# Sliding-window attention and a gated feed-forward on one core: block 1 begun on three of its four tiles, tile 9 loaded ahead of wo, and unit 7's divisions put before masks

## The chip, the cores and the metric

The kernel runs on one core of a Trainium2 chip. The metric is the device time of one launch in microseconds (us). Before the change it is 340.84 us, the median of three runs that lie between 340.82 and 340.93 us.

## What is computed

Eight batches of causal attention with eight heads, 576 positions of 64 numbers, a window of 128 and a bias that falls with distance; then a gated feed-forward over all 4608 rows.

```python
q, k, v: (8, 8, 576, 64)            # batch, head, position, dim
scores = q @ k.T / 8 + slope[h] * -abs(i - j)
scores = where((i - j >= 0) & (i - j < 128), scores, -1e9)
attn   = softmax(scores) @ v
x      = attn.transpose(0, 2, 1, 3).reshape(4608, 512)
g      = x @ w_gate                 # 512 -> 1536
out    = (silu(g) * (x @ w_val)) @ w_out    # 1536 -> 512
```

Inputs and output are float32 in memory. The kernel converts the inputs to float16 while they are loaded, and accumulates in float32.

## The kernel before, in words

**Units and blocks.** Attention is done in 36 units: for each pair of batches eight tiles of 128 positions and one tile that holds the last 64 positions of both. A unit's x is 128 rows of 512. The feed-forward works on nine blocks of 512 rows. Block 0 takes units 0 to 3, block 1 units 4 to 7; unit 8 goes to the last block, and unit 9 opens the second pair of batches. For a block, `wide` (L394) forms for each of twelve slices of the hidden width a gate tile `pg` and a value tile `pv`: four matmuls of 128x512 each, over the four parts of the contraction. ScalarE then takes a tanh (L420), VectorE makes `uu` (L421) and multiplies by `pv` into `hT` (L432). Blocks 0 and 1 have `gate_val`'s two steps per slice, so 24 steps are block 0. Block 0 is projected with wo by `project` (L451, twelve matmuls per 128 rows); later blocks by a scheme with seven products instead of eight.

**One unit.** Its q and k tiles are loaded by GpSimd as 128 rows, transposed on TensorE (L214, the DMA's transpose from rank 11 on), and multiplied (L282, or L318 for the units with half-width tiles). ScalarE takes the exponential, VectorE multiplies by a mask (L294, L326). `weighted` (L330) multiplies by v into two halves `av` (L350) and divides: a reciprocal (L352) and a multiplication (L353) for each half. `x_transposed` (L363) transposes x on TensorE (`px`, L376), and ScalarE copies it into the block's `xT` (L380). With that a tile of the block is there.

**PSUM.** The eight banks are split: three for the tag "gv" (gate and value tiles after the start), one for "po" (projections of block 0), four for "a" (scores, av, transposes).

**Begun tiles.** Block 0's first four gate and value tiles are begun by `begin` (L819) on the columns of the tiles that are there: `wide` with a column limit leaves the half-made tile in `early`, and the later call computes only the columns that are left.

**What sets the order.** The loads on GpSimd's queue are in program order, written out by hand (L886 to L920): q, k, v tiles among the slices of the gate and value weights, then v of tile 8, then the two halves of wo (L913, L914; the second half of its rows first), then k and q of tile 9, q of tile 10 and the rest. TensorE, VectorE and ScalarE run in program order up to the eighth step of block 0. From there to step 60 the compiler's list scheduler chooses the order of each engine: it takes the earliest instruction in program order that its own model of time holds to be ready. After step 60 TensorE is again in program order. The order that results is fixed before the kernel runs; on the chip an engine that waits for one instruction doesn't go on to the next. Program order puts the whole chain of unit 7 and the scores of unit 8 ahead of block 1, since `ready` (L925) asks for eight finished units before the sixth step from the end of block 0.

Of the kernel before, what the change touches and what calls it, by code (L numbers as in the profile page):

```python
# [16 lines left out]
P = 128  # L17
# [21 lines left out]
def slot(h):  # L39

    return 4 * (h // 4) + 2 * (h % 2) + (h % 4) // 2
# [9 lines left out]
def kernel(  # L51
# [10 lines left out]
    nc = tc.nc  # L62
    B, H, S, D = q.shape
# [105 lines left out]
    def source(src, rank):  # L169

        s, c = divmod(rank, 9)
        if c == 8:
            return [((64 * n, 64 * n + 64),
                     src[2 * s + n, :, 512:576, :].rearrange("h p d -> p h d")) for n in range(2)]
        b, t = 2 * s + c // 4, c % 4
        return [((0, P), src[b, :, t * P:(t + 1) * P, :].rearrange("h p d -> p h d"))]

    def load_v(rank):
        va[rank] = va_all[rank % NV]
        for (p0, p1), src in source(v, rank):  # L180
            nc.gpsimd.dma_start(va[rank][p0:p1, :, 0:D], src)  # L181

    def load_qk(rank, which="kq"):
        for name in which:
            t_ = nat.tile([P, H, D], FP16, name=name + "n", tag=name + "n")
            for (p0, p1), src in source(k if name == "k" else q, rank):
                nc.gpsimd.dma_start(t_[p0:p1], src)  # L187
            (natk if name == "k" else natq)[rank] = t_

    def load(rank):  # L190
        load_qk(rank)
        load_v(rank)
# [137 lines left out]
    def weighted(i):  # L330

        s, p = units[i]
        x = xpool.tile([P, H, D], FP16, name="x", tag="x")
        xs[i] = x
        for half in range(2):
            pool, tag = (ps_f, "gv") if i < FIRST else (ps_a, "a")
            av = pool.tile([P, 4, D + 1], FP32, name="av", tag=tag)
            todo = []
            for j in range(4):
                h = 4 * half + j  # L340
                if p == 8:
                    for n, kt in enumerate((3, 7, 8)):
                        todo.append((j, ex[(s, "c", n)][:, slot(h), :], va[9 * s + kt][:, h, :]))
                else:
                    if p not in (0, 4):
                        todo.append((j, ex[(s, p - 1)][:, slot(h), 128:256],
                                     va[9 * s + p - 1][:, h, :]))
                    todo.append((j, ex[(s, p)][:, slot(h), 0:128], va[9 * s + p][:, h, :]))
            for n, (j, w, val) in enumerate(todo):
                nc.tensor.matmul(av[:, j, :], w, val, start=(n == 0), stop=(n == len(todo) - 1))  # L350
            rec = xpool.tile([P, 4, 1], FP32, name="rec", tag="rec", bufs=4)
            nc.vector.reciprocal(rec, av[:, :, D:D + 1])  # L352
            nc.vector.tensor_mul(x[:, 4 * half:4 * half + 4, :], av[:, :, 0:D],  # L353
                                 rec.broadcast_to([P, 4, D]))

    xT = {}

# [33 lines left out]
    early = {}  # L391
    OTHER = {(0, 0, "g"), (0, 0, "v"), (0, 1, "g"), (0, 1, "v")}

    def wide(n, m, which, c1=512):  # L394

        w, ms = wg_sb if which == "g" else wv_sb, slice(m * P, (m + 1) * P)
        ps, c0 = early.pop((n, m, which), (None, 0))
        if ps is None:
            pool, tag = (ps_a, "a") if (n, m, which) in OTHER else (ps_f, "gv")
            ps = pool.tile([P, 512], FP32, name="p" + which, tag=tag)  # L400
        for kb in range(NKB):
            nc.tensor.matmul(ps[:, c0:c1], w[:, kb, ms], xT[n][:, kb, c0:c1],  # L402
                             start=(kb == 0 and c0 == 0), stop=(kb == NKB - 1 and c1 == 512),
                             skip_group_check=(n == 0))
        if c1 < 512:
            early[(n, m, which)] = (ps, c1)
        return ps
# [87 lines left out]
    def at_once(fs):  # L495
        for f in fs:
            f()
# [208 lines left out]
    def ffn():  # L706

        for n in range(NBLK):
            if n > 1:
                parts = chain(strassen(n - 1, 0), strassen(n - 1, 1))  # L710
            if n == 1:
                for j in range(PRE):
                    for _ in project(0, j, ps_f, "po", 1):
                        yield 1.0
            if n == SEVEN_FROM:
                break
            due, given = 0, 0
            for m in range(NMB):
                for half, _ in enumerate(gate_val(n, m)):
                    scored[0] = False  # L720
                    yield 1.0
                    due += n > 1 and 2 * m + half in AT
                    while due and not (scored[0] and given % 7 == 1):
                        next(parts)
                        due, given = due - 1, given + 1
                        yield 0.75
                    if n > 1:
                        for _ in range(1 + (len(later) > 3)):
                            if later:
                                later.pop(0)()  # L730
                if n == 1:
                    if m in (4, 6, 8, 10):
                        for _ in project(0, m // 2 - 2, ps_f, "po", 1):
                            yield 1.0
                    if m in (4, 6, 8):
                        weight_sums(m // 2 - 2)
                if n > 0 and m >= 9:
                    (at_once if n == 1 and m < 11 else later.extend)(sums(n, m - 9))
                if n + 1 == SEVEN_FROM:
                    if m == SILU_AT:  # L740
                        attention_ends()
                        by_silu.update((n, i) for i in range(m + 1, NMB))
                    if m in (SILU_AT + 1, SILU_AT + 2):
                        later.extend(gate_val_weight_sums(m - SILU_AT - 1))
                    if m == SILU_AT:
                        later.extend(x_sums(n + 1))
            if n > 1:
                assert next(parts, 0) == 0
        ends = [strassen(NBLK - 1, t) for t in range(2)]
        tail = ExitStack()  # L750
        for n, k, name, which in seven_steps():
            if k == 0 and n > SEVEN_FROM:
                assert next(parts, 0) == 0
                parts = chain(strassen(n - 1, 0), strassen(n - 1, 1))
            if n == SEVEN_FROM and k in (1, 3, 10, 17):
                later.extend(gate_val_weight_sums(2 + (k + 4) // 7))
            yield 0.5
            if k % 3 == 2 and k < 42:
                next(parts)
                yield 0.75  # L760
            if k == 20 and n + 1 < NBLK:
                later.extend(x_sums(n + 1))
            if k == 35:
                later.extend(sums(n, 0))
            if name == "fourth" and which is not None and which[1] > 3:
                if n + 1 < NBLK or k < 39:
                    later.extend(sums(which[0], which[1] - 3))
            for _ in range(2 if len(later) > 4 or k < 7 else 1):
                if later:
                    later.pop(0)()  # L770
            if n == NBLK - 1 and k == 38:
                at_once(later)
                later.clear()
                tail.enter_context(tc.manual_schedule(engines={ET.DVE}))
            if n == NBLK - 1 and k == 39:
                one, two = sums(n, 1), sums(n, 2)
                one[0]()
            if n == NBLK - 1 and k == 41:
                one[1]()
                next(ends[0])  # L780
                yield 0.75
            if n == NBLK - 1 and k == 42:
                two[0]()
        assert next(parts, 0) == 0 and not later
        at_once((two[1], one[2], two[2], one[3], two[3]))

        for t in (1, 0, 1, 0, 1, 0, 1, 0, 0, 1, 0, 1, 1):
            next(ends[t])
            yield 0.75
        tail.close()  # L790
# [25 lines left out]
                f()  # L816
            yield

    def begin(n, tiles):  # L819

        for m, which in ((0, "g"), (0, "v"), (1, "g"), (1, "v"), (2, "g"), (2, "v"))[:n]:
            if early.get((0, m, which), (None, 0))[1] < tiles * P:
                wide(0, m, which, tiles * P)

    def first_tiles():

# [83 lines left out]
    load_w(1280, 1536)  # L910
    load_v(7)
    load(8)
    nc.gpsimd.dma_start(wo_sb[:, 6:12, :], wo2[:, 6:12, :])  # L913
    nc.gpsimd.dma_start(wo_sb[:, 0:6, :], wo2[:, 0:6, :])  # L914
    load_qk(9)
    load_qk(10, "q")
    load_v(9)
    load_qk(10, "k")
    load_v(10)
# [94 lines left out]
```

The softmax here doesn't subtract the row's maximum and nothing guards it: scores larger than these inputs give would overflow.

## Time and profile before

| engine | busy us | share of the span |
|---|---|---|
| TensorE matmuls | 328.6 | 97% |
| VectorE | 274.7 | 81% |
| ScalarE | 208.3 | 61% |
| GpSimd | 109.7 | 32% |

The profiled span is 339.4 us, with a mean granted TensorE clock of 0.997. The chain that ended last lies 79% on TensorE and 11% on DMA. The page gives each engine's busy time and then cuts the span in 40 slices; a stretch of the trace can be asked for the busy time of each engine in it, and the timeline gives each instruction's start, its length, and in brackets the idle time of the engine before it with what ended it. Idle time counts only on the engine that sets the end. A matmul's recorded length is longer than its share of the stream, since matmuls overlap: four of 128x512 take 0.86 us from the start of one group to the start of the next.

### The profile page before, as it was taken

To read this page: it belongs to the slowest core of one execution; us is meant where nothing else is said; L and a number is where in the kernel's file an instruction comes from. 1 tells how busy PE (TensorE), PEld (TensorE's weight loads), DVE (VectorE), ACT (ScalarE), POOL (GpSimd) and SP (SyncE) were. 2 spreads that over 40 slices of the span, in tenths; PEclk is the share of its full clock that TensorE was granted. 3 is DMA by queue.
4 is the path that set the end of the run, shared out by engine and by line. 5 is a ranking of instruction groups with operands and counts; after the bars stand their busy time and mean duration, and the time that the engine had idled before them with its cause. 6 is when DMAs were issued, how large, how long until landed. Compare 5 with 4: busy or idle time off the path is not lost.

```text
span 339.4 us, 7672 instructions
## 1 busy us (share of the span) xinstructions
PE 328.6 (97%) x2935; PEld 217.4 (64%) x2935; DVE 274.7 (81%) x643; ACT 208.3 (61%) x415; POOL 109.7 (32%) x136
## 2 busy tenths in 40 slices
PE   8999987999999999999999999999999999999994
PEld 4564444444455665566665655666688888888884
DVE  4668874999888779998899999999955885776683
ACT  4866774555575676666665647563467776776650
POOL 8977675377837068743008000000000000000000
PEclk9999999999999999999999999999999999999998
DMA  9999999999999999999939913021101101011014
GB/s 151 169 178 178 166 162 162 128 139 157 142 170 147 172 153 179 157 156 154 181 109 109 152 39 93 17 58 53 62 2 64 47 17 65 0 65 62 2 64 125
DMA packets 160037, 37.37 MB, mean 110 GB/s; under 512 B 147328, under 2 KB 155648, under 8 KB 160000
## 3 DMA queue, kind: packets, MB, share of 16 engines
q0 software_dynamic: 118336, 18.62, 80.3%
q1 hardware_dynamic: 40976, 17.64, 28.4%
q10 hardware_dynamic: 688, 0.62, 0.6%
q8 instruction: 23, 0.38, 0.5%
q14 instruction: 14, 0.11, 0.1%
HBM read 37.91 MB, written 9.44 MB: 139 GB/s over the span
## 4 chain that ended last, share of the span: by engine, by line
PE 79%; DMA 11%; POOL 4%; DVE 2%; ACT 2%; issue 1%; POOLq 0%
PE po L537 19%; PE pg L402 15%; PE pv L402 15%; PE gX L626 9%; DMA wv_sb<-in_moe_w_val_dram 5%; PE gY L626 5%; PE av L350 4%; DMA qn<-in_q_dram 3%; PE ps L282 3%; PE p L537 3%; DMA va<-in_v_dram 3%; PE gZ L626 2%; PE po L456 2%; POOL va L181 1%; PE px L376 1%
## 5 line engine op out<-in xcount | busy, mean ns | idle before, releaser
L402 PE MATMUL pv<-xT,wv_sb 128*128 128x512 f16 (+2 forms) x304 | 75.8, 368 | 0.3 <-DVE uu L421 0.3
L402 PE MATMUL pg<-xT,wg_sb 128*128 128x512 f16 (+2 forms) x304 | 75.1, 368 | 0.2 <-DVE xT L378 0.2
L420 ACT ACTIVATE tt<-pg 128x512 f16<-128x512 f32 x68 | 41.0, 603 | 47.2 <-PE pg L402 46.9
L288 ACT ACTIVATE ex<-ps 128x512 f16<-128x512 f32 x96 | 49.9, 606 | 7.5 <-PE ps L282 7.5
L421 DVE SCALAR_TENSOR_TENSOR uu<-tt,pg 128x512 f16<-128x512 f16 x67 | 45.6, 680 | 9.1 <-ACT tt L420 9.1
L432 DVE TENSOR_TENSOR hT<-uu,pv 128x512 f16<-128x512 f16 x68 | 46.2, 680 | 2.9 <-PE pv L402 1.3
L181 POOL DMA_DIRECT2D va<-in_v_dram x40 | 34.3, 865 | 42.3 <-PE av L350 34.6
L537 PEld LDWEIGHTS <-hT 128*128 128x128 f16 x384 | 37.2, 98 | 10.6 <-issue 0.8
L402 PEld LDWEIGHTS <-wv_sb 128*128 128x128 f16 x304 | 27.3, 98 | 24.8 <-issue 2.7
L402 PEld LDWEIGHTS <-wg_sb 128*128 128x128 f16 x304 | 27.3, 98 | 23.2 <-issue 1.9
L187 POOL DMA_DIRECT2D kn<-in_k_dram x39 | 33.3, 858 | 16.8 <-DMA qT<-qn 6.4
L187 POOL DMA_DIRECT2D qn<-in_q_dram x39 | 33.4, 865 | 12.6 <-DMA va<-in_v_dram 5.4
L537 PEld LDWEIGHTS <-S 128*128 128x128 f16 x288 | 27.4, 98 | 7.3 <-issue 1.4
L294 DVE TENSOR_TENSOR ex<-ex,m_reg 128x1024 f16<-128x1024 f16 x42 | 28.7, 685 | 2.6 <-ACT ex L288 2.5
L353 DVE TENSOR_TENSOR x<-av,rec 128x256 f16<-128x256 f32 x72 | 28.7, 419 | 0.4
L537 PE MATMUL po<-T,S 128*128 128x256 f16 x192 | 25.9, 273 | 0.3 <-ACT u2s L563 0.3
L537 PE MATMUL po<-T,hT 128*128 128x256 f16 x192 | 26.0, 272 | 0.0
L322 ACT ACTIVATE exc<-psc 128x512 f16<-128x512 f32 x40 | 21.3, 607 | 1.9 <-PE psc L318 1.9
L680 DVE TENSOR_TENSOR hT<-s,v 128x512 f16<-128x512 f16 x18 | 7.6, 424 | 17.7 <-ACT s L679 17.7
L350 PEld LDWEIGHTS <-ex 128*128 128x128 f16 x384 | 17.4, 97 | 3.9 <-issue 0.4
L350 PE MATMUL av<-va,ex 128*128 128x65 f16 x384 | 19.3, 193 | 0.0
L282 PE MATMUL ps<-qT,kT 64*128 64x256 f16 x192 | 16.9, 272 | 0.3 <-DVE qT L219 0.2
(130 smaller groups left out, 535.3 us busy)
## 6 DMA issues: line engine op xcount, KB each, us to landing
out_dram<-osb SPq DMA_DIRECT2D x32, 256.0 KB, 2.1
va<-in_v_dram POOLq DMA_DIRECT2D x32, 128.0 KB, 7.8
qn<-in_q_dram POOLq DMA_DIRECT2D x31, 128.0 KB, 8.1
kn<-in_k_dram POOLq DMA_DIRECT2D x31, 128.0 KB, 8.8
wg_sb<-in_moe_w_gate_dram POOLq DMA_DIRECT2D x6, 256.0 KB, 7.7
wv_sb<-in_moe_w_val_dram POOLq DMA_DIRECT2D x6, 256.0 KB, 8.1
wo_sb<-in_moe_w_out_dram POOLq DMA_DIRECT2D x2, 768.0 KB, 10.4
kn<-in_k_dram POOLq DMA_DIRECT2D x8, 64.0 KB, 6.0
```

The source lines that it names most:

```text
L181: nc.gpsimd.dma_start(va[rank][p0:p1, :, 0:D], src)
L187: nc.gpsimd.dma_start(t_[p0:p1], src)
L288: nc.scalar.activation(e[:, o:o + 2, :], banks[q4][par], AF.Exp, scale=scale)
L294: nc.vector.tensor_mul(e[:, o, :], e[:, o, :], reg[:, o, :])
L350: nc.tensor.matmul(av[:, j, :], w, val, start=(n == 0), stop=(n == len(todo) - 1))
L353: nc.vector.tensor_mul(x[:, 4 * half:4 * half + 4, :], av[:, :, 0:D], rec.broadcast_to([P, 4, D]))
L402: nc.tensor.matmul(ps[:, c0:c1], w[:, kb, ms], xT[n][:, kb, c0:c1], start=(kb == 0 and c0 == 0), stop=(kb == NKB - 1 and c1 == 512), skip_ ...
L420: nc.scalar.activation(tt, pg[:, c0:c1], AF.Tanh, scale=0.5)
L421: nc.vector.scalar_tensor_tensor(out=uu, in0=tt, scalar=one if (n, m) == PIN else 1.0, in1=pg[:, c0:c1], op0=ALU.add, op1=ALU.mult)
L432: nc.vector.tensor_mul(hT[n][:, m, c0:c1], acted[(n, m)][1][:, c0:c1], pv[:, c0:c1])
L537: nc.tensor.matmul(dst, a[:, m, cols], b[:, m, :], start=(start and m == 0), stop=(m == HM - 1), skip_group_check=True)
L626: nc.tensor.matmul(dst[:, i, :], w[:, kb, c0 + i * P:c0 + (i + 1) * P], a[:, kb, :], start=(start and i == 0 and kb == 0), stop=(i == 1 an ...
```

## The change

Three edits aim at the end of block 0, where the first two blocks meet. (1) When block 1 opens, three of its tiles (the gate and value tiles of slice 0 and the gate tile of slice 1) are begun on the 384 columns of units 4, 5 and 6. The last 128 columns follow when unit 7's x is there. (2) k and q of tile 9 and q of tile 10 are loaded ahead of wo instead of behind it. (3) The reciprocals and multiplications of unit 7 are given high priority in the scheduler, so that the mask multiplications of unit 8's scores don't come between them.

```diff
@@ weighted
             rec = xpool.tile([P, 4, 1], FP32, name="rec", tag="rec", bufs=4)
-            nc.vector.reciprocal(rec, av[:, :, D:D + 1])
-            nc.vector.tensor_mul(x[:, 4 * half:4 * half + 4, :], av[:, :, 0:D],
-                                 rec.broadcast_to([P, 4, D]))
+            with tc.high_priority() if i == 7 else ExitStack():
+                nc.vector.reciprocal(rec, av[:, :, D:D + 1])
+                nc.vector.tensor_mul(x[:, 4 * half:4 * half + 4, :], av[:, :, 0:D],
+                                     rec.broadcast_to([P, 4, D]))
@@ wide
-                             skip_group_check=(n == 0))
+                             skip_group_check=(n <= 1))
@@ ffn
             if n == 1:
+                begin(3, 3, 1)
@@ begin
-    def begin(n, tiles):
+    def begin(n, tiles, block=0):
 
         for m, which in ((0, "g"), (0, "v"), (1, "g"), (1, "v"), (2, "g"), (2, "v"))[:n]:
-            if early.get((0, m, which), (None, 0))[1] < tiles * P:
-                wide(0, m, which, tiles * P)
+            if early.get((block, m, which), (None, 0))[1] < tiles * P:
+                wide(block, m, which, tiles * P)
@@ the loads
     load(8)
+    load_qk(9)
+    load_qk(10, "q")
     nc.gpsimd.dma_start(wo_sb[:, 6:12, :], wo2[:, 6:12, :])
     nc.gpsimd.dma_start(wo_sb[:, 0:6, :], wo2[:, 0:6, :])
-    load_qk(9)
-    load_qk(10, "q")
     load_v(9)
```

## Prediction

> **What bounds the kernel now.** I read the page first, then the busy time by stretch, then TensorE's timeline where it is idle, then VectorE's there.
>
> From the page:
>
> ```profile
> span 339.4 us, 7672 instructions
> PE 328.6 (97%) x2935; PEld 217.4 (64%) x2935; DVE 274.7 (81%) x643; ACT 208.3 (61%) x415; POOL 109.7 (32%) x136
> ```
>
> TensorE is busy 97%, so 339.4 - 328.6 = 10.8 us of idle time is all that reordering could win. Where it lies, by stretch (columns: stretch, length, busy us and count of PE, PEld, DVE, ACT, POOL, then clock, DMA share, GB/s):
>
> ```profile
> 47.00:50.00 3.00, 1.86 (x29) 1.34 (x29) 2.25 (x6) 2.08 (x5) 1.38 (x2) 1.00 1.10 162
> 50.00:54.00 4.00, 2.99 (x32) 1.53 (x31) 2.94 (x7) 2.24 (x5) 0.88 (x1) 1.00 1.79 178
> 54.00:57.30 3.30, 2.48 (x22) 1.38 (x21) 0.68 (x2) 1.17 (x2) 2.86 (x4) 1.00 2.43 155
> 57.30:65.00 7.70, 7.70 (x38) 3.21 (x37) 6.01 (x12) 4.06 (x7) 1.51 (x2) 1.00 2.05 153
> ```
>
> From 47 to 57.3 us TensorE is idle 1.14 + 1.01 + 0.82 = 2.97 us, at full clock. From 57.3 to 338 us, asked as one stretch, it is busy 277.19 of 280.70 us. So what is won before 57.3 us should reach the end nearly whole. The timeline there (start, length, instruction; in brackets the idle time before it and what ended it):
>
> ```profile
> 49.97 0.38 PE L456 MATMUL po<-wo_sb,hT 128*128 128x512 f16 x1 [0.26 <-DMA wo_sb<-in_moe_w_out_dram]
> ...
> 53.78 0.59 PE L456 MATMUL po<-wo_sb,hT 128*128 128x512 f16 x2 [1.01 <-DMA wo_sb<-in_moe_w_out_dram]
> 54.21 0.27 PE L376 MATMUL px<-idm,x 128*128 128x128 f16 x2
> 54.74 0.40 PE L214 MATMUL pt<-idm,kn 128*128 128x128 f16 x4 [0.26 <-DMA kn<-in_k_dram]
> 55.70 0.40 PE L214 MATMUL pt<-idm,qn 128*128 128x128 f16 x4 [0.56 <-DMA qn<-in_q_dram]
> 55.94 0.59 PE L456 MATMUL po<-wo_sb,hT 128*128 128x512 f16 x2
> 56.37 0.28 PE L376 MATMUL px<-idm,x 128*128 128x128 f16 x2
> ...
> 57.32 1.02 PE L402 MATMUL pg<-xT,wg_sb 128*128 128x512 f16 x4
> ```
>
> Block 1 starts at 57.32 because its fourth tile is unit 7's x, whose second half of transposes (56.37) stands behind fillers that wait for DMA: projections of block 0 for wo, transposes of tile 9 for k and q. Four waits, 0.26 + 1.01 + 0.26 + 0.56 = 2.09 us, are for transfers that nothing urgent needs. VectorE at that time:
>
> ```profile
> 52.38 0.18 DVE L352 RECIPROCAL rec<-av 128x4 f32<-128x4 f32 x1 [0.28 <-PE av L350]
> 52.48 0.39 DVE L353 TENSOR_TENSOR x<-av,rec 128x256 f16<-128x256 f32 x1
> 52.79 0.68 DVE L326 TENSOR_TENSOR exc<-exc,m_c 128x1024 f16<-128x1024 f16 x1
> 53.39 0.42 DVE L353 TENSOR_TENSOR x<-av,rec 128x256 f16<-128x256 f32 x1
> ```
>
> A mask of 0.68 us stands between the two halves of unit 7's x.
>
> **What the skill says.** The Trainium skill's "TensorE: Matmul & The Clock Gate" ("Step-by-step: what each phase is for") says that matmuls stay in program order and only weight loads are pulled ahead. The trace agrees: px at 56.37 waits behind pt at 55.70, though x was done at 53.81. "DMA: Bandwidth & Descriptors" ("Queues, rings and completion order") says that each DMA engine consumes one ring's descriptors in order. The trace agrees: issue plus landing time gives wo's halves at 40.67 + 9.3 = 49.97 and 42.30 + 11.4 = 53.70, k of tile 9 at 43.12 + 11.6 = 54.7, then q of 9 and 10 at 55.7 and 56.6. "PSUM — Partial Sum Buffer" ("The four PSUM rules") allows one matmul at most one bank; so three tiles begun are all three "gv" banks, and the fourth has to wait for one.
>
> **The change, part by part.**
>
> *Splitting the three tiles.* Twelve matmuls of 512 columns become twelve of 384 and twelve of 128. In block 0 groups of four start 0.44 us apart at 256 columns and 0.22 at 128, in block 1 0.86 at 512: 110, 55 and 216 ns each. So 384 is about 163 ns, and 163 + 55 = 218 against 216: no cost, 12 x 2 ns. Twelve more weight loads (98 ns each) overlap; the groups at 128 columns show that they already do.
>
> *Whether the begun part may run before unit 7's x is written.* It reads columns 0 to 383 of xT and the copy writes 384 to 511, but the copy is earlier in program order. Block 0 shows that no false wait follows:
>
> ```profile
> 19.99 0.38 PE L376 MATMUL px<-idm,x 128*128 128x128 f16 x4 [0.52 <-DVE xT L378]
> 20.21 0.39 PE L402 MATMUL pg<-xT,wg_sb 128*128 128x128 f16 x4
> 20.41 0.42 DVE L378 COPY xT<-px 128x512 f16<-128x512 f16 x1 [0.47 <-PE px L376]
> ```
>
> The begun pg of tile 2 runs at 20.21, before the copy of tile 3 at 20.41. In block 1 the third tile (unit 6) is copied at 48.70 for 0.59 us, so from 49.3 on TensorE has 12 x 163 = 1.95 us of work that waits for no DMA. The "gv" banks are free by then: block 0's last pv starts at 46.50 and is read at 48.57 for 0.68 us.
>
> *Tile 9 ahead of wo.* The same bytes in another order. The three tiles are 0.95 us apart in landing, so wo's halves come 2.85 us later, at about 52.8 and 56.5, and k9, q9, q10 at about 47.1, 48.1 and 49.0 (wo's first half took 3.75 us of transfer, as the halves are 3.75 apart, so the slot begins near 46.2). The waits at 54.74 and 55.70 (0.82 us) go, and their 0.66 us of transposes can fill the idle time near 48. v9 and what follows land as before. GpSimd's queue gets no new wait that matters: its issues run 6 to 12 us ahead of landing.
>
> *Priority.* x's second half would start at about 52.8 and end at 53.2 instead of 53.81. The mask comes 0.35 us later; only unit 8 waits for it, which goes to the last block. Then px at about 53.4 and the copy (0.59) until about 54.3.
>
> *Sum.* From 49.34 to 57.32 there are 7.98 us, of which 2.09 are waits: 5.89 of work. Without the twelve projections (12 x 0.216 = 2.59) 3.30 remain; with the begun matmuls 3.30 + 1.95 = 5.25. So TensorE is done at about 54.6, just after x is there at 54.3, and block 1's rest starts 2.72 us earlier. It has 1.95 us done and 2.59 us of projection yet to do: net 2.72 + 1.95 - 2.59 = 2.08, the removed waits again.
>
> *The wait that it adds.* The fourth tile (pv of slice 1) wants a bank 12 x 0.055 = 0.66 us after the rest starts. Before, pg's first matmul started at 57.32 and uu, which frees the bank, ended at 59.76, 1.42 us after pg's end (58.34). Now pg's rest ends 0.39 us in, so the bank comes at 0.39 + 1.42 = 1.81: a gap of 1.15 us. What stands behind is all of block 1. Bounds: 0, if projections (2.59 us, if wo has landed) or scores of unit 9 (0.61 us, with k9 and q9 there) fill it; 1.15 if nothing does. I take 0.4.
>
> So 2.09 - 0.4 = 1.7 us: 340.84 - 1.7 = 339.1 us.
>
> **The rivals.**
>
> *A filler still waits for wo.* The scheduler placed projections ahead of px by a model that held wo to be there 0.3 to 1.0 us too early. If the first projections of the second half stay ahead of px, TensorE waits for wo until 56.5 instead of 53.78 and the rest starts about 58.2 (56.5 + 0.86 of projections and transposes + 0.8 for px and its copy). 1.95 us is done by then, 0.9 is lost: gain about 1.05, 339.8 us. For it: both waits for wo stand in the trace. Against: the begun tiles precede projections in program order.
>
> *The gain is given back in block 1.* The bank gap stays open (-1.15), and a wait of 0.7 us for wo: 2.09 - 1.85 = 0.2, 340.6 us. For it: VectorE is busy 14.67 of 15.00 us from 65 to 80, so it has no room to catch up on late evictions. Against: VectorE is busy only 0.68 us of 54.00 to 57.30 and could start the evictions some 3 us earlier.
>
> *Slower.* All orders after step 8 of block 0 come from one list schedule, and on VectorE and ScalarE to the end. TensorE's idle time after 57.3 is small (3.5 us with the tail), so a new order can hardly be better there and may be worse. If it opens the 1.15 us gap and waits as large as the largest now (1.01, and 0.82 for the two transposes), 2.98 us, the result is 340.84 - 2.09 + 2.98 = 341.7 us. For it: VectorE's share. Against: no such wait stands in TensorE's waits now; the longest after 57.3 is 0.3.
>
> **How the numbers follow.** First case 0.55 (339.1); waits for wo 0.18 (339.8); given back 0.16 (340.6); slower 0.11 (341.7). Within 0.2% is 340.16 to 341.52. The first two are faster, less a little that spills: 0.71; the third and the spill: 0.18; slower 0.11. The range reaches down to 338.3 (all of 2.09 and 0.4 more, from transposes in the idle 1.14 us near 48) and up to 341.0, through the third case.
>
> **What would show it.** Right: pg and pv of 128x384 from about 49.3; transposes of tile 9 before 50 with no wait for DMA; x's second half straight after the first; pg of 128x128 near 54.6; TensorE's idle time from 47 to 57.3 at about 1 us, and none new behind. Wrong: the begun matmuls waiting for unit 7's copy, a wait for wo ahead of px, an idle gap ended by uu at the fourth tile, or new idle time from 60 to 250 us.

## The result, and the profile after

The changed kernel takes 338.48 us (median of four runs, 338.2 to 339.0) against 340.88 us before (340.82 to 341.01): 2.40 us less, a ratio of 0.9931 with a 95% interval from 0.9913 to 0.9948. Forecast were 339.1 us and a range from 338.3 to 341.0. On another chip, beside some of the experiments, the same kernel took 338.52 us against 340.54: 2.02 us less, 0.9938 (0.9926 to 0.9949).

The profiled execution after is the slowest of its four (339.0 us). Its page:

```profile
span 337.2 us, 7693 instructions
PE 328.0 (97%) x2947; PEld 217.8 (65%) x2947; DVE 274.3 (81%) x643; ACT 208.0 (62%) x415; POOL 109.8 (33%) x136
```

Twelve matmuls more (2947 against 2935), as the three split tiles ask, and idle time of 337.2 - 328.0 = 9.2 us against 10.8. By stretch, columns as before (stretch, length, busy us and count of PE, PEld, DVE, ACT, POOL, clock, DMA share, GB/s):

```profile
47.00:50.00 3.00, 2.29 (x33) 1.57 (x33) 2.08 (x5) 2.07 (x6) 3.00 (x5) 1.00 0.83 94
50.00:54.00 4.00, 3.94 (x52) 2.83 (x50) 3.20 (x8) 2.85 (x7) 1.68 (x2) 1.00 1.22 204
54.00:57.30 3.30, 3.30 (x26) 1.83 (x25) 2.48 (x5) 1.35 (x3) 0.88 (x1) 1.00 1.54 193
57.30:65.00 7.70, 7.04 (x37) 2.76 (x36) 6.84 (x15) 3.85 (x7) 1.75 (x2) 1.00 2.26 150
```

From 47 to 57.3 us TensorE now idles 0.71 + 0.06 + 0 = 0.77 us, where it idled 2.97. A new 0.66 us is idle between 57.3 and 65. The DMA moves 94 GB/s from 47 to 50, where it moved 162. TensorE's timeline:

```profile
49.48 0.34 PE L403 MATMUL pg<-xT,wg_sb 128*128 128x384 f16 x1
...
52.63 0.28 PE L377 MATMUL px<-idm,x 128*128 128x128 f16 x2
52.74 0.33 PE L403 MATMUL pg<-xT,wg_sb 128*128 128x384 f16 x1
52.90 0.28 PE L377 MATMUL px<-idm,x 128*128 128x128 f16 x2
53.01 0.39 PE L214 MATMUL pt<-idm,kn 128*128 128x128 f16 x4
...
53.85 0.38 PE L403 MATMUL pg<-xT,wg_sb 128*128 128x128 f16 x4
...
54.57 1.24 PE L457 MATMUL po<-wo_sb,hT 128*128 128x512 f16 x5
55.70 1.02 PE L403 MATMUL pv<-xT,wv_sb 128*128 128x512 f16 x4
...
60.30 1.02 PE L403 MATMUL pv<-xT,wv_sb 128*128 128x512 f16 x4 [0.66 <-DVE uu L422]
```

The begun matmuls start at 49.48 in the gaps where projections stood, unit 7's transposes run at 52.63 and 52.90 (54.21 and 56.37 before), tile 9's follow without a bracket, and block 1's rest starts at 53.85 instead of 57.32. Five projections fill the time in which the fourth tile waits for its bank (54.57 to 55.70). VectorE:

```profile
51.95 0.74 DVE L354 TENSOR_TENSOR x<-av,rec 128x256 f16<-128x256 f32 x2
52.61 0.68 DVE L326 TENSOR_TENSOR exc<-exc,m_c 128x1024 f16<-128x1024 f16 x1
...
54.90 0.75 DVE L422 SCALAR_TENSOR_TENSOR uu<-tt,one,pg 128x512 f16<-128x512 f16 x1 [0.82 <-ACT tt L421]
...
58.90 0.75 DVE L481 SCALAR_TENSOR_TENSOR T<-wo_sb,one 128x512 f16<-128x512 f16 x1 [0.77 <-DMA wo_sb<-in_moe_w_out_dram]
59.56 0.68 DVE L422 SCALAR_TENSOR_TENSOR uu<-tt,pg 128x512 f16<-128x512 f16 x1
```

Both halves of x run as one pair, then the mask. The `uu` at 54.90 frees the first of the three banks. At 58.90 a sum of two parts of wo (the scheme with seven products needs such sums) waits 0.77 us for wo's second half, and the next `uu` stands behind it; that is where TensorE's 0.66 us comes from.

### The profile page after: what moved, and what is told of

Same layout as the page of the kernel before. It is cut to its first block, busy times and chain, and to the rows that moved or that the text cites. A ratio compares the mean times of both kernels' runs of the same rounds, so it can differ in the third digit from the quotient of the medians.

```text
span 337.2 us, 7693 instructions
## 1 busy us (share of the span) xinstructions
PE 328.0 (97%) x2947; PEld 217.8 (65%) x2947; DVE 274.3 (81%) x643; ACT 208.0 (62%) x415; POOL 109.8 (33%) x136
## 4 chain that ended last, share of the span: by engine, by line
PE 83%; DMA 8%; DVE 3%; POOL 2%; ACT 1%; issue 1%; DVEq 0%; POOLq 0%
PE po L538 19%; PE pv L403 15%; PE pg L403 15%; PE gX L627 9%; PE gY L627 5%; PE av L350 4%; DMA wo_sb<-in_moe_w_out_dram 4%; PE ps L282 4%; PE p L538 3%; PE po L457 3%; DMA va<-in_v_dram 3%; PE gZ L627 2%; DMA qn<-in_q_dram 2%; PE px L377 1%; PE psc L318 1%
## 5 line engine op out<-in xcount | busy, mean ns | idle before, releaser
L403 PE MATMUL pv<-xT,wv_sb 128*128 128x512 f16 (+3 forms) x308 | 76.1, 365 | 1.0 <-DVE uu L422 0.9
L403 PE MATMUL pg<-xT,wg_sb 128*128 128x512 f16 (+3 forms) x312 | 76.0, 363 | 0.3 <-DVE xT L379 0.2
```

## The experiments

**Each edit alone, and pairs.** Each time was taken beside the kernel before on the same chip. The first four rows are from one chip, where the kernel before takes 340.60 us, the last two from another, where it takes 340.54. Rows of different chips are compared by their ratios.

| edits | time, us | ratio to before | 95% interval |
|---|---|---|---|
| begun tiles | 340.00 | 0.9987 | 0.9975 to 0.9999 |
| load order | 345.46 | 1.0142 | 1.0127 to 1.0157 |
| priority | 341.02 | 1.0016 | 1.0007 to 1.0025 |
| begun tiles, load order | 338.72 | 0.9951 | 0.9939 to 0.9963 |
| begun tiles, priority | 340.41 | 1.0000 | 0.9984 to 1.0016 |
| all three | 338.52 | 0.9938 | 0.9926 to 0.9949 |

What makes the table readable: moving the loads leaves TensorE's instruction order as it was, row for row in the traces, in each pair that differs by the load order alone. Such a pair differs only in when the data is there.

*The begun tiles alone* (the hunks in `wide`, `ffn` and `begin`; the line that matters):

```diff
+                begin(3, 3, 1)
```

> Only the first edit: block 1 begun on three tiles; the loads and the divisions as before. Theory A (the waits in front of unit 7's x are what was won, each edit taking its own): the begun matmuls replace the projections as filler, so the two waits for wo (1.27 us) go, and the waits for k and q of tile 9 (0.82 us) stay. Gain about 1.1 us, 339.8 us. Rival B (the order of the loads did it all, the begun tiles only trade places with projections): no gain, 340.9 us.

Measured: 340.00 us, 0.6 us below the 340.6 of before; theory A's direction, about half its size. Against rival B the interval speaks only just. The waits for wo are gone from TensorE's list, but tile 9's are there, and in this trace they are three: k for 0.34 us, q for 0.56, and q of tile 10 for 0.19.

*The load order alone:*

```diff
+    load_qk(9)
+    load_qk(10, "q")
     nc.gpsimd.dma_start(wo_sb[:, 6:12, :], wo2[:, 6:12, :])
     nc.gpsimd.dma_start(wo_sb[:, 0:6, :], wo2[:, 0:6, :])
-    load_qk(9)
-    load_qk(10, "q")
```

> Only the second edit: k and q of tile 9 and q of tile 10 ahead of wo. Theory A: the waits for k and q (0.82 us) go, but projections are then the only filler and wo lands about 2.8 us later, so a wait for wo grows ahead of unit 7's x: between 0.3 us faster and 2 us slower, about 341.7 us. Rival B: the load order is what was won, so about 2 us faster, 338.9 us.

Measured: 345.46 us, 4.9 us slower. Rival B is out. Theory A has the cause and not the size. TensorE's timeline, then its busy time by stretch (stretch, length, PE busy and count, granted clock, DMA share, GB/s):

```profile
49.31 0.38 PE L318 MATMUL psc<-qT,kT 64*128 64x128 f16 x7 [0.20 <-ACT xT L380]
53.89 0.59 PE L456 MATMUL po<-wo_sb,hT 128*128 128x512 f16 x1 [4.20 <-DMA wo_sb<-in_moe_w_out_dram]
54.41 0.60 PE L318 MATMUL psc<-qT,kT 64*128 64x128 f16 x4
```

```profile
50.00:54.00 4.00, 0.11 (x1) 0.81 1.24 206
54.00:57.30 3.30, 3.30 (x21) 0.50 1.60 189
57.30:65.00 7.70, 7.68 (x50) 0.87 2.24 149
```

A projection, a filler, stands ahead of unit 8's last scores and of unit 7's av. It waits 4.20 us, and the whole chain waits with it. After the idle time the granted clock is 0.50. Block 1 starts at 61.34, 4.02 us later than before. The three tiles moved ahead hurt because the filler that needs wo kept its place.

*The priority alone* (the line that matters):

```diff
+            with tc.high_priority() if i == 7 else ExitStack():
```

> Only the third edit: the reciprocals and multiplications of unit 7 have priority. Theory A: x's second half is done 0.6 us earlier, but its transposes stand behind those of tile 9, which wait for their loads until 55.7 us: no difference, 340.9 us. Rival C (the mask between the halves was on the path): 0.5 us faster, 340.3 us.

Measured: 341.02 us, nothing won and by the interval 0.07 to 0.25% lost. Rival C is out. The profile (of a run at 340.63 us, below the median) shows what took over:

```profile
54.59 0.40 PE L214 MATMUL pt<-idm,qn 128*128 128x128 f16 x4 [0.45 <-DMA qn<-in_q_dram]
55.52 0.40 PE L214 MATMUL pt<-idm,qn 128*128 128x128 f16 x4 [0.53 <-DMA qn<-in_q_dram]
55.75 0.81 PE L457 MATMUL po<-wo_sb,hT 128*128 128x512 f16 x3
56.40 1.03 PE L403 MATMUL pg<-xT,wg_sb 128*128 128x512 f16 x4
```

Unit 7's x comes sooner, but q of tile 10, the last of the three to land, stands ahead of block 1. Why the time is a little longer, and not the same, isn't shown.

*Begun tiles and load order, without the priority:*

> The first and second edits without the priority. Theory A: all four waits go, and unit 7's x comes 0.6 us later than with the priority. Block 1's rest then starts up to 0.6 us later, with the transposes of tile 9 or a projection in between as filler: 0.2 to 0.6 us slower than all three together, 338.7 to 339.1 us. Rival B: as the load order alone.

Measured: 338.72 us. TensorE's timeline:

```profile
53.85 0.38 PE L456 MATMUL po<-wo_sb,hT 128*128 128x512 f16 x1 [0.16 <-DMA wo_sb<-in_moe_w_out_dram]
54.07 0.27 PE L376 MATMUL px<-idm,x 128*128 128x128 f16 x2
...
55.02 0.38 PE L402 MATMUL pg<-xT,wg_sb 128*128 128x128 f16 x4
```

Without the priority a projection still stands ahead of the second half of unit 7's transposes, and waits 0.16 us for wo. The rest of block 1 starts at 55.02, against 54.03 in a trace of all three from another chip, but three projections (0.65 us) are done by then. The interval overlaps that of all three, so the priority's own share, about 0.13% by the two ratios, isn't settled.

*All three again, and all three but for the load order:*

> The changed kernel again, beside the next three on one chip: 338.2 to 338.9 us by every theory.

> The first and third edits, with the loads as before. Theory A (each edit takes its own waits): unit 7's transposes no longer stand behind those of tile 9, since x is done in time, but the transposes of tile 9 still wait for their loads ahead of block 1's rest: about 0.8 us slower than the whole change, 339.4 us. Rival D (with the priority the load order no longer matters, since x passes the late tiles): as the whole change, 338.6 us.

Measured: 338.52 and 340.41 us. TensorE's order is the same in both; the load order is worth 1.9 us here. Rival D is out, and theory A, with its 0.8 us, was too small. The trace of the kernel with the old loads:

```profile
54.49 0.40 PE L214 MATMUL pt<-idm,qn 128*128 128x128 f16 x4 [0.56 <-DMA qn<-in_q_dram]
55.42 0.34 PE L214 MATMUL pt<-idm,qn 128*128 128x128 f16 x3 [0.54 <-DMA qn<-in_q_dram]
55.60 0.39 PE L403 MATMUL pg<-xT,wg_sb 128*128 128x128 f16 x4
```

The last of unit 7's transposes start at 53.17, and then TensorE waits for three landings in turn. The rest of block 1 starts at 55.60 against 54.03. The kernel before hardly waited for the third (its transposes start at 56.61 and could have at 56.48), since it came late to it. What a removed wait gains is limited by the next landing in the same order.

**How much must be begun.**

```diff
-                begin(3, 3, 1)
+                begin(2, 3, 1)
```

> The whole change with two tiles begun instead of three. Theory A (the begun matmuls are the filler that keeps projections from waiting for wo in front of unit 7's x): with 0.65 us less of it two projections come ahead of unit 7's transposes and wait for wo, which lands near 53.5 us: 0.7 to 1.2 us slower than the whole change, 339.5 us. Rival (any filler before the projections is enough): 338.5 us.

Measured: 339.97 us, 0.9978 (0.9970 to 0.9987): between before and all three. As theory A has it, two projections come ahead of unit 7's transposes:

```profile
53.04 0.59 PE L457 MATMUL po<-wo_sb,hT 128*128 128x512 f16 x2 [0.63 <-DMA wo_sb<-in_moe_w_out_dram]
53.47 0.27 PE L377 MATMUL px<-idm,x 128*128 128x128 f16 x2
```

The cost by the ratios, 0.40% or 1.4 us, is somewhat more than the 0.7 to 1.2 expected; the intervals allow both. With the priority, the third tile is what keeps the order clear of wo until unit 7 is through.

**Where wo may land.** Two more load orders under TensorE's same order. The first, against the changed kernel:

```diff
     load(8)
+    nc.gpsimd.dma_start(wo_sb[:, 6:12, :], wo2[:, 6:12, :])
     load_qk(9)
     load_qk(10, "q")
-    nc.gpsimd.dma_start(wo_sb[:, 6:12, :], wo2[:, 6:12, :])
     nc.gpsimd.dma_start(wo_sb[:, 0:6, :], wo2[:, 0:6, :])
```

The second puts both halves of wo behind v of tile 9 and k and v of tile 10.

> The whole change, but tile 9's k and q and tile 10's q are loaded between the two halves of wo. TensorE's order is the same. Theory H (only the landing times against this fixed order count): the first half of wo lands near 50, the three tiles near 51 to 53, just before their transposes at 53.0 to 53.6: 338.5 us, at most 0.4 more. Rival (the three tiles must be ahead of all of wo): 339.5 us or more.

> The whole change, with wo behind three more tiles (v of 9, k and v of 10). TensorE's order is the same. Theory H: wo's first half lands 2.9 us later, near 56.5 us, and its first projection stands in TensorE's order at 54.8: a wait of about 1.7 us there, and the sums of wo's parts on VectorE wait for the second half near 60.2 us: 1.7 to 2.2 us slower than the whole change, 340.4 us. Rival (the transfers are hidden, since projections are only filler): 338.5 us.

With tile 9 between the halves: 338.71 us, 0.9942 (0.9923 to 0.9962), as all three. The tiles need not be ahead of all of wo. With wo behind three more tiles: 340.61 us, 1.0006 (0.9995 to 1.0016), the whole gain lost. Both times are as theory H said. The trace with wo last (of a run at 341.21 us, above the median), TensorE and then VectorE:

```profile
56.44 1.24 PE L457 MATMUL po<-wo_sb,hT 128*128 128x512 f16 x5 [0.95 <-DMA wo_sb<-in_moe_w_out_dram]
```

```profile
60.84 0.75 DVE L481 SCALAR_TENSOR_TENSOR T<-wo_sb,one 128x512 f16<-128x512 f16 x1 [0.89 <-DMA wo_sb<-in_moe_w_out_dram]
```

The first is the filler's wait, for which theory H had 1.7 us; from start to start it is 1.12 (56.44 - 55.32). The second is the wait seen in the profile after, larger here, and TensorE waits 0.8 us for `uu` behind it: wo made later brings it back.

**The wait through VectorE.** `PIN` names the gate that has to be done before the sums of wo's parts may start.

```diff
-    PIN = (1, 0)
+    PIN = (1, 3)
```

> The whole change, but the first sums of wo's parts on VectorE may not run before the gate of slice 3 of block 1, instead of slice 0 (their scalar is held until then). Theory E: the one new wait of 0.66 us on TensorE, which uu ended, comes from such a sum that stands ahead of uu on VectorE and waits for wo. With the sum later the wait goes: 0.5 to 0.7 us faster than the whole change, 337.9 us. Rival F: the wait is for a PSUM bank that VectorE couldn't empty sooner anyway, so it stays: 338.5 us.

> As the one before, and the divisions of unit 6 have priority as well. Theory A: the two waits of TensorE for unit 6's x (0.57 and 0.20 us) stand before the begun matmuls; a mask of 0.68 us lies between the halves, so the second wait goes and the begun matmuls start up to 0.3 us earlier: 337.6 us. Rival: the scores behind them wait for copies and banks of their own, so nothing is won: 337.9 us.

Measured: 338.83 and 338.85 us, both 0.9944 (0.9932 to 0.9957 and to 0.9956): nothing won. The wait that was to go isn't in the trace of all three on this chip either, where wo's second half lands at 57.3 us and the sum runs at 58.23 without waiting; so the expected gain wasn't there to be had. The later sums put VectorE in another order, in which unit 8's x comes later:

```profile
66.47 0.28 PE L377 MATMUL px<-idm,x 128*128 128x128 f16 x2 [0.45 <-DVE x L354]
```

With unit 6's divisions put first as well, the wait of 0.20 us for its second half goes, and one of 0.52 us for the copy of tile 8's q takes its place in front of the scores.

**Why wo lands so late.** Against the changed kernel:

```diff
-    load(8)
+    load_qk(8)
     load_qk(9)
     load_qk(10, "q")
     nc.gpsimd.dma_start(wo_sb[:, 6:12, :], wo2[:, 6:12, :])
     nc.gpsimd.dma_start(wo_sb[:, 0:6, :], wo2[:, 0:6, :])
+    load_v(8)
```

> The whole change, with v of tile 8 (needed near 65 us) behind wo. Theory G: GpSimd never has more than eight loads under way, and the six small ones of tile 8 left the DMA with little to do from 43 to 49 us; with wo issued 2 us sooner it lands near 52 us. Time: the late wait on VectorE for wo can't occur, so the runs lie at 338.2 to 338.5 us, 0 to 0.3 us faster. Rival (the transfer rate, not the issue, set wo's landing): wo about 0.9 us earlier by v's bytes alone, the same time.

Measured: 338.63 us, 0.9938 (0.9917 to 0.9959): the same time as all three, and none of the gain that theory G allowed. The landing moved the way theory G said, and further than its 52 us. The rows of the wo tile around its issue, in this kernel:

```profile
L917 POOL DMA_DIRECT2D wo_sb<-in_moe_w_out_dram x1: 818/818/818, 42.0 to 42.0; - x1
L918 POOL DMA_DIRECT2D wo_sb<-in_moe_w_out_dram x1: 826/826/826, 42.8 to 42.8; - x1
...
DMA to landing us min/median/max: 8.4/10.1/11.8
```

The first half lands at 42.0 + 8.4 = 50.4 us, against 44.1 + 9.4 = 53.5 with all three as they are. One tile out of the way is worth 0.95 us of transfer; the other 2.1 us match the earlier issue (42.0 instead of 44.1). In this program a load waits for the one eight issues earlier, as GpSimd's timeline of the kernel before shows:

```profile
50.46 0.88 POOL L187 DMA_DIRECT2D kn<-in_k_dram  x1 [2.08 <-DMA wo_sb<-in_moe_w_out_dram]
54.03 0.87 POOL L187 DMA_DIRECT2D qn<-in_q_dram  x1 [2.68 <-DMA wo_sb<-in_moe_w_out_dram]
```

Each is the eighth load after one half of wo, which land at 49.97 and 53.70. In the changed kernel the eight loads ahead of wo are five of 64 KB, of tile 8, and three of 128 KB, and from 42 to 48 us the DMA moves 57 to 109 GB/s in the trace of all three; with v of tile 8 behind wo it moves 86 to 193. How much of that is the limit of eight, and how much the 0.68 us that GpSimd takes to issue a load of 64 KB, isn't separated. This didn't set the time, since projections ask for wo only at 54.8.

No version tried beats the changed kernel.

## Why the prediction was right

**What bounds the kernel.** Right: after the two blocks meet, the gain is carried to the end. The first of the products that end a block starts at 97.3 us before and 94.9 after, the last at 334.9 and 332.6. From block 1's start to the end it is 282.08 us before and 282.67 in the profile of all three on the other chip; the difference is about the 0.64 us of work (2.59 - 1.95) that now stands behind this point instead of ahead of it.

**Splitting costs nothing; no false wait follows.** Right: the begun matmuls run from 49.48, forecast 49.3.

**Tile 9 ahead of wo.** Right that the waits go; too simple in "the same bytes in another order". wo landed at 44.77 + 9.1 = 53.9 and 45.58 + 13.2 = 58.8 instead of 52.8 and 56.5. Its issue slid by 4.1 and 3.3 us: the three loads take 0.87 us each to issue, and GpSimd waits 1.19 us before the first and 0.91 us after it. The second half also took 13.2 us from issue to landing, where it took 11.4. The prediction put GpSimd's queue at nothing; the late landing came to 0.66 us through VectorE in this execution.

**Priority.** Right in place: x is done at 52.69, forecast 53.2. Counted from the scores (49.34 before, 49.17 after) it is 0.34 us sooner than forecast, about the first wait for wo, which this step had left in. Alone the priority brings nothing.

**The sum.** The step that was mis-sized is the 2.09 us of waits. The idle time in brackets counts from the modelled end of the last matmul, which is later than the moment when the next could have started: a 128x512 matmul is recorded with 0.38 us, and the next starts 0.216 us after it. From start to start: in the changed kernel the begun matmul follows the seven score matmuls 0.31 us after their start (49.17 to 49.48), so before, TensorE could have gone on at 49.34 + 0.31 = 49.65 and did at 49.97; the two projections at 52.18 leave 53.78 - 52.61; then 54.74 - 54.32 and 55.70 - 54.96. That is 0.32 + 1.17 + 0.42 + 0.74 = 2.65 us, 0.56 more. It is why block 1's rest starts at 53.85 to 54.03 rather than 54.6: from the scores to there it takes 4.68 us after (49.17 to 53.85) and took 7.98 before, 3.30 less where 2.72 were forecast. By profiles, 2.7 us were won between the one before (339.4 us span) and that of all three on the other chip (336.7). The medians differ by less, 2.0 to 2.4 us; the profiled run before was at 341.2 us, 0.4 above its median. How long the waits for wo are differs by execution: with the loads in the same order wo's halves landed at 48.7 and 52.6 us in the profile of the priority alone, and at 49.97 and 53.70 in the one that the forecast was made from.

**The added wait.** Forecast 0.4 us for a bank at the fourth tile. The bank comes when the prediction had it: `uu` ends at 54.90 + 0.75 = 55.65, and 1.81 us after the rest's start is 55.66. But projections fill the gap: from 54.57, five at 0.216 us end at 55.65, and pv starts at 55.70. The wait that appeared is another one, 0.66 us for wo at 60.30. That the term came near its size is luck.

**The rivals.** A filler that waits for wo is real. It is what the load order alone shows, at 4.20 us, what two begun tiles show, at 0.63, and what three begun tiles without the priority show, at 0.16; with all three edits it isn't there ahead of unit 7's transposes. VectorE gave nothing back beyond the 0.66, and no other new idle time opened: from 65 to 100 us TensorE idles 0.10 us, 0.33 before.

**The pieces don't add.** By medians the three edits alone are worth -0.6, +4.9 and +0.4 us, together -2.0. The prediction costed them together, in one order, and so didn't depend on such a sum. The expectations that split the waits between the edits missed: 0.8 us for the load order was 1.9 with the begun tiles, and a loss of 4.9 without.

## What to carry to other kernels

Where an engine's order is fixed ahead, cost an edit by going through that order with new landing times, not by adding up idle times by their causes: a filler ahead of the critical chain turns a late transfer into a stall of the whole chain. So give the gap work that needs no transfer first, and only then move the transfer. And measure a gap on TensorE from start to start.

## What the runs showed of the hardware

One wait of 4.20 us of TensorE cost more than its length. In the kernel with the load order alone the granted clock fell to 0.50 at 52.5 us and stayed there until 59.3, while in the kernel before, whose longest wait in this place is 1.01 us, it stayed at 1.00. At 0.50 four projections take 1.65 us (57.75 to 59.40), 0.41 each instead of 0.216. The Trainium skill's "TensorE: Matmul & The Clock Gate" ("What's actually happening") says that the clock is halved after an idle window of about 3.4 us. This trace agrees with the halving; the fall came 2.8 us after the idle time began at 49.69, sooner than the page's figure.

TensorE works from 53.89 to 59.3 at half the clock, 5.4 us for what takes 2.7 at 1.00. By that estimate 2.7 of the 4.9 us of the loss are the clock, and the longer wait alone would have cost about 2.
